# Three mask copies moved from VectorE to DMA, split output blocks at the end, and a new written-out order in a fused attention and gated-convolution kernel

## The chip, the cores and the metric

The kernel runs on one core of one Trainium2 chip. The core has five engines that run side by side, each strictly through its own list of instructions: TensorE (PE: matmuls and transposes), ScalarE (ACT: exponentials and other activations, copies), VectorE (DVE: elementwise work, copies), GpSimd (POOL: here the issue of the casting loads) and SyncE (SP: here the issue of the other DMAs). Engines wait for one another by semaphores. The metric is the device time of one execution in microseconds (us).

## The reference, cut to what matters

Block-sparse attention (4 batches, 8 heads, 768 tokens, head size 64, blocks of 32 tokens), and then a gated convolution feed-forward on the 512 wide result:

```python
scores = scale * q @ k.T
mask   = |blk_i - blk_j| <= 1, or first/last block on either side, or one of 3 sampled blocks of the query's block
attn   = softmax(where(mask, scores, -1e9));  x = attn @ v        # heads side by side: 4 x 768 x 512
h      = relu(x @ w_in)                                           # 512 -> 1024
conv   = sum over k of conv_w[k] * h shifted by k - 1 tokens      # 3 taps, per channel
out    = (h * sigmoid(conv)) @ w_out                              # 1024 -> 512
```

## The kernel before, in words

The 8 heads of a batch go as 4 pairs, so there are 16 pairs, P = 0 to 15. A pair's queries and keys lie transposed in a tile `T_t[slot]` of 88 rows by 24 columns of 128: rows 0 to 63 hold q and k, rows 64 to 87 hold the mask as 24 more "head elements" (a large negative number where a block pair is masked), so that one matmul over 88 rows gives the masked scores. There are five such slots. The mask rows are built once, in slot 0, by small DVE and ACT instructions at the start (`a1`, `a3`, `nblk`, `m_k`, `a4`, `a5`, `m_q0`, `m_q1`, `m_h1`, `m_r1`; lines 270 to 350), and copied from there into slots 1 to 4 by four VectorE copies `m_slot` (lines 354 to 357). Pair P uses slot P modulo 5 at first; pairs 1, 2, 3 are needed 4.5, 9 and 13.5 units after pair 0, pair 4 only 36 units after it.

The attention is 144 units. One unit is two `s` steps on TensorE (line 761: 1024 columns of scores into one of two PSUM tiles `st`), one `exp` on ScalarE (line 773: 128 x 1024 elements), and two `av` steps on TensorE (line 798). Every 18 units (one segment, half the tokens of a batch) the normalised rows (`rcp`, `norm`) are transposed (`x_tr` on TensorE or `x_xb` by DMA), multiplied with w_in (`f1`, line 895), cut at zero (`relu`, on ACT or DVE), convolved and gated on DVE with a `tanh` on ACT (`mul`, `add`, `tanh`, `g1`, `g2`), and multiplied with w_out (`f2`, line 830). A finished block of 128 tokens by 512 columns is copied out of PSUM by `ev` (ACT or DVE, function `dcopy`, lines 327 and 331) and stored by SP's `out` (line 839). Only the very last block, token block 5 of batch 3, is done in two halves of 256 columns, in the score tiles.

At the head, pair 0's q and k are loaded in fp32: q of head 0 first on ACT's queue, k of head 0 first on SP's. They are cast to bf16 (`cast_q`, `cast_k`), transposed on TensorE (`k_tr`, `q_tr`) and copied into slot 0 (`k_cp`, `q_cp`). Until the first scores TensorE is kept busy with 13 `warm` and 29 `fill` matmuls on zeros. All other loads go through POOL's casting queue, in a chain that is paced by tiny POOL copies (`pace`).

No scheduler decides the order: a function builds a list of 1787 operations with their choices of engine and of buffers, and the string `ORDER` (lines 20 to 62) gives, operation after operation, its number (two characters), the engine where there is a choice, and the buffers that it takes. `put_down` emits them so. The sequence of each engine is what this string leaves for it; the waits between engines follow from the data.

Of the kernel before, what the change touches and what calls it, by code (L numbers as in the profile page):

```python
# [21 lines left out]
1B01H10ZA0YA1CV01d1e1IA0+A13A0p0q1DV1E00r0s0t0u1FV1L01a1GV15V550560v0w0x5701yV165a15b0y0z0A0B2005c1222230C1J00D  # L22
0E0F0G1PA01Y12e11KV1S12a22g32h2s25f05g5h25k11V05l580595d1TV11UV1WV1XV5p05q0O1M15e1h05m35i5r4175y15z1i1n1NV1OV5j
5n5o21V15A55D05E2402715F05I15J5K10H25V228V29V26V5s5t15N05O5B5C5G5W15X5H5L5P25Y35u05v5/0602i1614641656655M5Q2l0
6906a2fV2186b05R5Z05+2jV32kV2mV2nV6e16f6g15w162636n0195S15T6o67686c6d6s16t5xV06p26u36h6x06y2u12tV36i16q6r4P2v4Q
2o34R1r2G04S2I01s1g4T2J4U6C16D6j26k6v1Z06l16z46L06M1l1p1+V6mV1/V6E51m1t4V2U14W1u4X2W24Y2X4Z1v4+6w6A6B6Q16R6F6N0
6G5U16S16V06W6X21w4/312506O06P6H06I6J05VV6T6+16/6KVih11k73074ii703ik01q2HV4ijV001o7547c17dil7e5in1ioipA17h07i
7m1imViF0iH7j0iGiIiq06U7n7o12b1ir2dV2cVisA7r06Y7s6Z7172767717A17B11iz1iA2Z07t27F07G7f7C32w0iBA2iJiN1iO7H4782iQ
797g7K12p12xV47L2rV2yV7k7l7p2qV7M57P07Q7qit02z17u7viP2BV2AV7w1iR7R07U17V7D0810iKiL7W12K12LV02MV7x82iuivV37E7I7J
7N8618733351347a17O7S7bV1832iS8838b07T7X7Z07Y18c7y08d4iT7+7zViM0iUiw1ixiyViV28g18h2Y1842N0858i58p08q8r0898a8u1  # L30
8v8e8f8j8k8w13522+361372OV2PViW8l28z08A8s08tiY8B27/18E18F8xiC08J08K8y80ViX8m8G38CiD8L48R18SiZ8T52VV0iEVj13j3j2
j918W08Xja8Y08n08D8H8/1908I9408M8oVi+8N1j42/V30Vj5911958U8V8Z8+jf096292jgi/j012j69c1j7j88O18P32V1939d9h09i97jh
jb9e49m19njijjV09j5jc9o139V38V523cjdA19r0989909a9s9w1jo0jp9t3jl11jjqA9x9E0jm9F3d13f9y09G2ju0jv3a0532C0542Q13e
9J19f09g3o3p03l3m1jwA9KjnVjJ0jK9k9O09P9l2D19pjL9L4jM2EV9Q5jr09q9ujs9vjN2FV3r3qjOjtVjR1jS3bV2jT9T19U9V1jA1jBjU
jx0jyjCAjzAjZ29/0a02R1a41a59z9B29A19H9I9M9N9R2TVa13a90aa9CjG08Q2j+jVk09ba602SAab2ae1afag4jD1jP9SjEjFVaj0akjH9W
jQj/jIVjk3h03t13i9D9Xa209Y19Za3k53k1al5jWa7a8acar1jXk6asaw0kj1axat3adahaiamaB1aCan1ay0auavazjYaD4k2kv0aG0aHk8
aI5k7k9ao0k3k4kaaO1kbkcaAkkaPaEaFkwaJaT0aKaL2aMaUkl3x3y23A3B2aQ1kxaY1aV29+3u3s4ap3g3aq03jV3kVkykzA2kmaZb103D3C
3Jb2knA3kB0kCkE1kFkDV14kGVkZ0k+a+3b303vVb61b7b84kN0kObe0aR1bfkQ1kRaSaWaXk/kPA5bj1bkkK0bg5kSAbl1l0l1l2kLbo0kW1a/
bpb0b4b5bt1b9buba0bq33M3N33K0aNbhld1kMVbv2kXbB0bCbikH0kYAbD03wVlf3nA3bG1kIbb1lelg3zV4bckT1bmbnbr3P3OkJV6bH3UbI4
3F03Q13Gl52l7kUkVV7l3bL0bMl6bN5kp0kqbsbwbxbQ1bRbS1bV0bWbdkokrkd1bE1bX33R3E0ll3lml8lol9lhlal41by0kAlblcbzlnlilp  # L40
ljc11ksbFbJbKbOc2c60c7c82ktA0bPbTbAkulk3IV3HVkekfkgc30cb0bUbYlt0lubZ0cccg1khA3lqlr3LV0b+2lscd4lvlz1chlAco0cplB
lCci5lwct1cuc4cq3lDA2lxA0cy0czc5lF13V23X3Y1403Zb/3+lGcv13SV13WV13TVlHVlI0lJcD1c9cElKVm10m2m3cacem4m5cA0cF2lO1cf
cI0cJcK4kilPlL0lMcjcklNAlQVm92ma410mbmcm6m7cl1cr1cQ1cRcS5cscwcV0cWcxcBcCcGcHlR0494a0c01ly4f1c+1c/cX13/46471cL
cN0mdd03lSd30d4lU1lVdb1dccOcmcncP42jelTAmelWVmh1mimjmfmkmgm84ed50dd2cM1cTcUcYcZlX0d1lYmllZVdg0dhdi4l+1l/dl1d2dm
d6d7dq0drm0Amp3de0d82dfdn54b4c4nds1mD1djdkdodpdv1dwdD0dEmx0mEmymmdx3mqd9msdtmrdudydz1dF2dI1dJmtmumnmo4o24s4ddG
dHdN0dOdK4mvmzmFdadP54kdS1dTdLmwmGdMd+0d/dQmA4pdA14l043V2mHV344VmBV0dU1e31dRe4e03dVdWdX0dBe52e80e9mV1mWea0mXV08
dYmY0mZe10e2m+Vnh0ninknjed1ee4glEn21e6m/0ei0ejn0n34B4C34qef4ek5n4A4Geq1ere7ebecegehelev04r4y4Des3n1V9np2nqnsnr
ewnl48V2en24hV3n50em1n6eteA1euex2n7Aa4t045dC2dZeBeon81mJ0eF0mKeGeC04z2n9mLnmeH4mMepeN1eOeS0eTmNA1naV4iV4mV34E4F
4MeP5ne1nb0nfeX1eyezeYeDeEeInx1nyntnzeU1nuf00eJncf1eZ34N14H1ngVnneK1eQ0eRmP1eVeWe+f514j4ueLeMf6f22ndAbe/f3fd0fe
f74mQmRnvno0nAnwnBnF3nGnInHfi1fjff5nCmC4vV4nD4wVnJf4mSmTA2nT0nUfn0fofk0f8f91fgo61o7fhfs1ftfp1fA0fBnK4Io8VnEmI  # L50
fu3nLfa0nMo31o4fC2flnVfmnWo5Vot0ouovowoxfb4AV4nXA0fF1fGfK0fLnN1nZ0nOfH4fM5oyfqfrnPn+n/AnQfP1fQo00fvo1nRA34JV0
4KVfwfU0fVoz4OV0oAfR0oc1g01g1o2AfW1fx2fyol2omfD0fEfIfJodonoog23opoeAg50g6g72o90oaga1fNfOfSgbfTfXfY1gf0ggobVoB1
oDoC4Loqgc4fZ1oi1ojof0ognS4xnYgh5orosoEf+g3g4gn1g8gogs0ohAokAoFoJ3oKg9gp0gtmUfc0fzoR0gu1oX1gdoLgegigx1gyoMoNoG
gjoSoHgG0gq0grgvgwgHoYgz3gAgBgL1gMoOgI2gk0oIglgC2gN4oToZgQ0gRgS5f/gmoPoQo+gJ1o/A3mOgZ1oUg+h20h3g/0h41p71p8p9pa
oVV0pbV2h71h8gKpg0phpd1p0pehg0gDgOpfV1cpiAhhh93pj0pm1pnhi2poAgPpkplAdhl1hmgThq0pp1gE0pqgUpB0pDpCpcpEpJ2pFhn4
gFA1h00h1h5h6haps0pthbprAepGpKpLpuAhrpMpv1hz1hApwhs5p10pHgV1gWhc0pNpxAfhB0hE0hdpR1pSpTpUp2gX1gYApOhj1hkp3p4hF
pI1pVp5A1hG1hohphthuhN1py1he0pzhv2pPhwhOhC0pQhfApAAhx0hDhHhW0hI1hyVqk1qlhP3hXpZ3hJ1p+p/pWqmAgqq0hQh/1qrhRq51hY2
i0i80i9q6q0q1pXhKq2qsAhpYhS0q3q4hL0q7hZ0q8i14ia5hMV2qh0qihTq9A3qB0qR2qCqDh+i2i31ibqn1qjAii42i5qt1qui60icid1qo
i7Aqb0qcqpAjqwqviehU1qdhVVif1qeigAri1rjqJ3qEqxqLqSqFqfA2r90raqyrkArbAqzqUrf1rgqGrc0rl0rmrhArA1rBp6qgoWqaqAqHqI
rn1qKrorC0rdr31rv0rwrDrpreArq1rrrEqTqMrx1rs0qZ0rtqNqOruryqVrzqPqQq+r4rR0rSrL1rMrNrOrTrUqWqXqYrPV1r5r6rVAr7A2q/  # L60
# [53 lines left out]
def kernel(  # L114
# [700 lines left out]

    def out_block(b, t, due, deps, after, tail=False, last=False):
        gb, ob = gt_buf[b], Buf(P_os)
        halves = ((0, 256), (256, 512)) if last else ((0, 512),)
        outs = []
        for x, (c0, c1) in enumerate(halves):  # L820
            mb = Buf(P_tail if last else P_mix)

# [4 lines left out]
            for a in range(4):
                def fn(e, a=a, acc=acc, c0=c0, c1=c1):
                    for ffc in (2 * a, 2 * a + 1):
                        nc.tensor.matmul(out=acc(), lhsT=gT_t[gb.index][:, ffc, 128 * t:128 * t + 128],  # L830
                                         rhs=woutb[:, ffc, c0:c1], start=(ffc == 0), stop=(ffc == NFFC - 1),
                                         skip_group_check=True)
# [224 lines left out]
```

## Time and profile before

| | |
|---|---|
| median of 3 runs | 208.67 us (208.65 to 208.9) |
| the profiled execution: span from first to last instruction | 206.8 us |
| what lies around the span, against the median | 1.9 us |
| PE, ACT, DVE, POOL busy | 199.3, 190.6, 186.4, 61.9 us |
| first `exp` starts, last `exp` ends | 7.61, 188.2 us |
| last matmul group starts, last copy out of PSUM ends | 199.4, 203.5 us |
| DMA | 25.2 MB, mean 122 GB/s |

The page shows the profiled execution by its span alone; its time is taken as this span and the 1.9 us around it. The page counts busy time by engine, gives the chain of work that ended last, and groups instructions by source line. A busy TensorE is not always one at its full rate, since the ends of its pipelined matmuls are modelled; its rate is better read from the chain of waits, where so many matmuls of one kind stand back to back with the time that they took.

### The profile page before, as it was taken

What the parts mean: (1) busy time and instruction counts of PE and PEld (TensorE: products, weight loads), DVE (VectorE), ACT (ScalarE), POOL (GpSimd) and SP (SyncE); (2) the same over time, 40 slices, a digit from 0 to 9 for tenths busy, and PEclk for the clock granted to TensorE, in tenths of its full rate; (3) what the DMA queues carried; (4) which work ended last, traced back from release to release, by engine and by line L of the source; (5) the groups of instructions that cost most, each with busy time, mean ns of one, the idle gap of its engine ahead of it and who ended that gap; (6) DMA issues with size and microseconds to landing.
All of it is one profiled execution on the core that took longest, in us unless ns stands there. A gap on an engine that the chain in (4) does not pass through costs nothing.

```text
span 206.8 us, 6250 instructions
## 1 busy us (share of the span) xinstructions
PE 199.3 (96%) x2418; PEld 142.7 (69%) x2418; DVE 186.4 (90%) x576; ACT 190.6 (92%) x252; POOL 61.9 (30%) x113
## 2 busy tenths in 40 slices
...
GB/s 156 196 196 185 181 165 132 187 113 77 78 127 142 179 102 93 147 139 193 194 96 107 138 77 170 151 144 130 67 115 87 22 120 51 3 51 5 152 53 153
DMA packets 49305, 25.20 MB, mean 122 GB/s; under 512 B 35100, under 2 KB 46332, under 8 KB 49276
## 3 DMA queue, kind: packets, MB, share of 16 engines
...
q10 hardware_dynamic: 288, 0.30, 0.4%
...
## 4 chain that ended last, share of the span: by engine, by line
PE 71%; DVE 14%; ACT 11%; issue 2%; ACTq 0%
PE st L761 22%; PE mix L830 18%; PE mix L895 16%; PE av L798 12%; ACT pt L773 8%; DVE t L331 3%; DVE m L953 3%; DVE m L961 2%; DVE gT L1008 1%; ACT t L327 1%; DVE xtok L709 1%; PE st L830 1%; DVE hE L917 1%; PE mix L728 1%; DVE m L1003 1%
## 5 line engine op out<-in xcount | busy, mean ns | idle before, releaser
L773 ACT ACTIVATE pt<-st 128x1024 bf16<-128x1024 f32 x144 | 140.6, 1048 | 2.4 <-PE st L761 1.3
L761 PE MATMUL st<-t 88*128 88x256 bf16 (+2 forms) x600 | 90.0, 267 | 1.6 <-ACT t L327 0.8
L761 PEld LDWEIGHTS <-t 88*128 88x128 bf16 x600 | 48.5, 97 | 21.4 <-issue 1.6
L798 PEld LDWEIGHTS <-pt 128*128 128x128 bf16 x1152 | 52.2, 97 | 11.5 <-ACT pt L773 1.0
L798 PE MATMUL av<-vt,pt 128*128 128x65 bf16 x1152 | 58.4, 193 | 0.0
L895 PE MATMUL mix<-xT,winb 128*128 128x384 bf16 (+2 forms) x288 | 54.3, 308 | 0.3 <-ACT hE L915 0.2
L953 DVE TENSOR_SCALAR m<-hE,cw 128x382 bf16<-128x382 bf16 (+2 forms) x192 | 48.8, 316 | 0.4
L830 PE MATMUL mix<-woutb,gT 128*128 128x512 bf16 x184 | 48.7, 379 | 0.2 <-DVE gT L1008 0.2
L961 DVE TENSOR_TENSOR m<-m 128x764 bf16<-128x764 bf16 (+2 forms) x64 | 33.8, 534 | 0.6
L895 PEld LDWEIGHTS <-winb 128*128 128x128 bf16 x288 | 24.4, 97 | 9.4 <-issue 0.8
L1000 ACT ACTIVATE m<-m 128x764 bf16<-128x764 bf16 (+2 forms) x32 | 26.8, 840 | 1.1 <-DVE m L961 1.0
L407 POOL COPY pace<-pt 1x1 bf16<-1x1 bf16 x24 | 9.6, 402 | 53.3 <-ACT pt L773 53.3
L830 PEld LDWEIGHTS <-gT 128*128 128x128 bf16 x200 | 17.3, 97 | 11.7 <-DVE gT L1008 1.1
L915 ACT ACTIVATE hE<-mix 128x384 bf16<-128x384 f32 (+2 forms) x36 | 17.7, 507 | 1.7 <-PE mix L895 1.6
L917 DVE TENSOR_SCALAR hE<-mix 128x384 bf16<-128x384 f32 x28 | 15.5, 557 | 4.1 <-PE mix L895 3.7
L1008 DVE TENSOR_TENSOR gT<-m,hE 128x764 bf16<-128x764 bf16 (+3 forms) x36 | 18.2, 511 | 0.6
L709 DVE TENSOR_TENSOR xtok<-av,rcp 128x384 bf16<-128x384 f32 (+2 forms) x36 | 18.1, 508 | 0.5
L239 POOL DMA_DIRECT2D nat<-in_q_dram x23 | 17.0, 738 | 2.1 <-issue 1.4
L331 DVE COPY t<-mix 64x384 bf16<-64x384 bf16 (+1 forms) x33 | 13.4, 413 | 0.7 <-PE mix L522 0.2
L327 ACT COPY o2s<-mix 128x512 f32<-128x512 f32 x17 | 9.9, 598 | 2.9 <-PE mix L830 2.7
L1003 DVE TENSOR_SCALAR m<-m 128x764 bf16<-128x764 bf16 (+3 forms) x36 | 12.1, 335 | 0.5 <-ACT m L1000 0.4
L239 POOL DMA_DIRECT2D vn<-in_v_dram x15 | 11.3, 756 | 1.9 <-DVE vt L331 1.4
...
## 6 DMA issues: line engine op xcount, KB each, us to landing
...
```

The costliest lines, as they stand in the source:

```text
L239: return op(name, {eng: occ}, lambda e: on(e).dma_start(out=dst(), in_=src), prio, deps, dma=(kind, service), **kw)
L331: nc.vector.tensor_copy(out=dst, in_=src)
L709: nm = op("norm", {"DVE": t_dps(128 * C)}, lambda e: nc.vector.tensor_tensor(out=xtok_t[xk.index][:, 0:C].rearrange("p c h d -> p h c d"), ...
L761: nc.tensor.matmul(out=st[:, 128 * x:128 * (x + n_)], lhsT=t[0:88, 12 + 6 * hh + kc, :], rhs=t[0:88, idx:idx + (n_ - 1) * (2 if P < NPE el ...
L773: nc.scalar.activation(out=pt_t[ptb.index][:, c0:c1], in_=st_t[stb.index][:, c0:c1], func=AF.Exp, bias=0.0, scale=0.125)
L798: nc.tensor.matmul(out=o[:, off:off + 65], lhsT=pt_t[ptb.index][:, 128 * x:128 * x + 128], rhs=V_t[vslot_b[P].index][:, hh, kc, 0:65], sta ...
L830: nc.tensor.matmul(out=acc(), lhsT=gT_t[gb.index][:, ffc, 128 * t:128 * t + 128], rhs=woutb[:, ffc, c0:c1], start=(ffc == 0), stop=(ffc == ...
L895: nc.tensor.matmul(out=mix_t[hb.index][:, w1 * y:w1 * y + w1], lhsT=winb[:, fc, 128 * ffc:128 * ffc + 128], rhs=xT_t[xt_buf[n].index][:, f ...
L953: nc.vector.tensor_scalar(out=m_t[cb.index][:, x, y, 0:w], in0=hE_t[heb.index][:, f0 + y, t0 + x:t0 + x + w], scalar1=cw[:, x, f0 + y:f0 + ...
L961: nc.vector.tensor_tensor(out=m[:, a_, :, 0:w], in0=m[:, a_, :, 0:w], in1=m[:, b_, :, 0:w], op=ALU.add)
L1000: th = [op("tanh", {"ACT": t_act(2 * w) + 0.04}, lambda e, cb=cb, w=w: nc.scalar.activation(out=m_t[cb.index][:, 0, :, 0:w], in_=m_t[cb.in ...
L1008: nc.vector.tensor_tensor(out=gT_t[gtb.index][:, f0:f0 + 2, t0:t1], in0=m_t[cb.index][:, 0, :, 0:w], in1=hE_t[heb.index][:, f0:f0 + 2, 1 + ...
```

## The change

First, `m_slot` stays a VectorE copy for slot 1 alone. For slots 2, 3 and 4 it becomes a DMA on SP's queue, `m_sp`, from slot 0's mask rows to the other slot's, 24 rows of 6144 bytes each (147 KB).

Second, blocks 3 and 4 of batch 3 are now also computed and stored in halves of 256 columns, as block 5 was. That makes 8 `f2` steps (32 matmuls of 256 columns in place of 16 of 512), 2 `ev` and 2 `out` more. These halves stay in the `mix` PSUM tiles.

Third, the whole `ORDER` is replaced (1799 operations). What it changes at the head, engine by engine (loads that the engine only issues are left out):

| engine | before | after |
|---|---|---|
| DVE | 3 fillers, memsets, a1, a3, nblk, m_k, ident24, m_h1, a4, a5, a5, k_cp ... | memsets, cast_q (head 0), a1, nblk, a3, m_k, ident24, a4, a5, k_cp, m_q0, cast_q, k_cp, m_h1, a5, q_cp, cw, m_q1, m_r1, m_slot, v_cp (pair 0), q_cp (pair 1), k_cp (pair 1) ... |
| ACT | m_k, cast_q, cast_k, cast_k, m_q0, m_q0, q_cp, m_q1, m_h1, exp 0, exp 1, v_cp (pair 0), exp 2, exp 3 ... | m_k, cast_k (head 1), cast_k (head 0), m_h1 (24 x 768), k_cp, q_cp, m_q0, k_cp, exp 0, exp 1, exp 2, k_cp and q_cp (pair 1), exp 3 ... |
| PE | 13 warm, 10 fill, k_tr 0, q_tr 0, 2 fill, k_tr 1, 4 fill, s 0, s 1 ... | 13 warm, 4 fill, k_tr 1, 7 fill, k_tr 0, q_tr 0, 11 fill, s 0, s 1, q_tr 1 ... |
| SP | mask to `mback` (2 DMAs), xb, m_turn ... | m_sp slot 2, mask to `mback` (2 DMAs), m_sp slot 3, m_sp slot 4, m_turn, xb ... |

On POOL both w_in loads now come before pair 4's q. Later in the run, ACT has 11 copies `o2s<-mix` of 512 columns where it had 17, and DVE 10 where it had 6; ACT no longer does the two `v_cp`, and DVE one `relu` fewer. In the last stretch TensorE ends with block 4 left, block 4 right and block 3 right, where it ended with block 3, block 2 and the whole block 4; the last copy is one of 256 columns on ACT.

```diff
 ORDER = """
-0J0K1c1f00021010P0Q1Q01R0R0S0T0310V0/A0U14V1b0I0L0M0N0V0W0X1xA11zA1AA0405060708090a0b0c0d0e0f0g0h0i0j0k0l0m0n0o
...
+00021030405060I0L0M0N0O010708090P0Q1Q01R0R0J0K1L00a1xV10R1b0T0S10V1d0U1a2000b0c0d0e0/A1AA0f0g0h0i1E00j0k0l0m0n0o0p1zA
...
 """
...
     for s in range(1, NSLOT):
-        mr = [op("m_slot", {"DVE": 0.95}, lambda e, s=s: dcopy(e, T_t[s][64:88], T_t[0][64:88]),
-                 T(4.5 * s - 2.5), m_h1 + m_r, earliest=7.0 + 2 * s)]
+        if s == 1:
+            mr = [op("m_slot", {"DVE": 0.95}, lambda e, s=s: dcopy(e, T_t[s][64:88], T_t[0][64:88]),
+                     T(4.5 * s - 2.5), m_h1 + m_r, earliest=7.0 + 2 * s)]
+        else:
+            mr = [dma("m_sp", "SP", lambda s=s: T_t[s][64:88].rearrange("j c s -> j (c s)"),
+                      T_t[0][64:88].rearrange("j c s -> j (c s)"), T(4.5 * s - 2.5), m_h1 + m_r, service=0.3)]
         mask_ready[(s, 0)] = mask_ready[(s, 1)] = mr
...
     def out_block(b, t, due, deps, after, tail=False, last=False):
         gb, ob = gt_buf[b], Buf(P_os)
-        halves = ((0, 256), (256, 512)) if last else ((0, 512),)
+        halves = ((0, 256), (256, 512)) if last or (b == B - 1 and t > 2) else ((0, 512),)
...
-                due + 3, [evo], uses=[ob], dma=("hw", 0.65 if not last else 0.4)))
+                due + 3, [evo], uses=[ob], dma=("hw", 0.65 if len(halves) == 1 else 0.4)))
```

More of the change, by code (lines that the diff above doesn't have):

```diff
@@ L20 @@
 ORDER = """
-0J0K1c1f00021010P0Q1Q01R0R0S0T0310V0/A0U14V1b0I0L0M0N0V0W0X1xA11zA1AA0405060708090a0b0c0d0e0f0g0h0i0j0k0l0m0n0o
[L22 to L60, printed above, removed]
@@ new lines @@
+5T1m6n06o1Z11+V2tV36p26c6d6s16t6x06y6h6j26k1/V6i16q6u36z46r6C16D6v6w6l06L06M6A6B5U15VV1g6mV6E56Q16R6F6G6N06S11w4/
+312506V06W6O06P6X26H06I1k6J16KV6+16/6T6Uih073074703ii7c17dik17547e5il7h02HV41qijV00imViF0iGiHiI7i7j0in0io7m17niq16Y
+6ZipA17o12b0ir7r07s712cV2dViJisA727t2iK762p17717A17BiN12qV2rV2w02xV47F07G7f7g7k7l7piO7822yV79iP7C37H4iz17q7uiA7K17L
+iBA27M57v2z07P07Q7D07E7I2K17U17V7w1iQ2AV2BV7R07J7N7O81082it07W133351342LV0iR2MViLiu86187iw17Six832iS883ivV37xiM0iyV
+7T7X7Z02VV08b08c7Y18d484852N08g18h8i57+2OV2PV898a7a18p08q7y08eiV27bV1iX7zViT2Y12Z02+iW2/ViY361352373g38r08f8u18v8j
@@ new lines @@
+7/18w18k8z08AiC08s08E18F8t8B28x8y8G38C8J08KiD8D8L48l280V8miZ32V1iEViU30Vj138R18S8T5j918W08X8Y08H8I8n08M8/1ja90940
+8N18U8V95i+8O1j28oVj3j4i/j538Vj039V911962j6jf0jg8Z8+929c19d939e4523a0533c3d12C03f543e9h09i97jbjh98j79m19nj8jijc990
+8P1jjjV09j39o59r09f09sjdA19t09w1jl0jm9xjo19a123bV2jnVjp9E0jqV9F9y19G2ju0jv9g9J19K2Q13l3o3p03m13r9k9l2D19O09PjwAjJ0
+jKjLjM9L49Q32EVjNjO2FV9pjr0js9q9ujtV9v9T19U9z9A19H9/0a0jA1jBjx09I9MjyjR19B2jSjTjU9C9V5a10a41a5jCAjzAa612R1a909Naa9R
+9S9W9Xa20ae1af3h08Q23q3i3t13u9bab2jVjZ22SVj+j/a3jG0jHaj0a7a8jP2TV9Y1k0ag4jWjIVakjD1acadahar1asal3aijEat0jQ9ZjXk1jFV
@@ new lines @@
+jYaw0aman1kj0axauaB1kv1aCkkk2ay1aG0aHavaD4kwazaAaO1aEaPaFaI3k53k6k7ao0k8k9kaaQ1aT0aJaKaUk3k4aV4klkx9+3s49Dkbkc3jVap
+3vVaL13A3B23x3D3M3N33y23CaY1kykzA2aZkmknV3b10a+5aR0b2kB1b32kCb61kE0kF3wVkDV14kGV3kVkZ0k+l0aMb7b803P3J3K0be0kH1bfkN0
+kOaSaWaXbj1a/kPA5b0kIb4b5bkb9kJV6bb2bg1bck/ba1bhbo0kQ0bpkRkSVbl3bq4bibmbt1bukW1bB0kXkK0bCbnbv5kYAld1le3nV3lglfbD2kL
+bG1brbHbI0bsbwkT1kUbL0bMkVA7bxbE0aq0je3E03F1aN3Q03Okojk3G3RbdbN1bFbQ1kp1kMVl1l52l23zV4ll3lhkd0bRbV0bJbKbObPkqbWkr
+bS3lic11bTksc2bX5ktA1c32l6lmby0lnl7l8bzl3l9l41lj3LV0lolklalbkebUbYkfc60lc3HVbAkuc7lz1cb1cckgbZ1c4c5c803X3Y13U3V140
```

26 lines of the change are left out of this document (25 added, 1 removed).

## The prediction

> **What bounds the kernel now.** I read the page first, then a table by stretches, cut at the first exp (7.61), at exp 24 (31.35), at exp 48 (57.86), and at the tail.
>
> ```profile
> PE 199.3 (96%) x2418; PEld 142.7 (69%) x2418; DVE 186.4 (90%) x576; ACT 190.6 (92%) x252; POOL 61.9 (30%) x113
> PE 71%; DVE 14%; ACT 11%; issue 2%; ACTq 0%
> ```
> ```profile
> core 0: us, PE busy (x) PEld busy (x) DVE busy (x) ACT busy (x) POOL busy (x), PEclk, DMA share, GB/s
> 0.00:7.61 7.61, 5.67 (x48) 4.43 (x49) 6.11 (x29) 5.21 (x11) 6.42 (x14) 1.00 0.77 169
> 7.61:31.35 23.74, 22.98 (x325) 18.02 (x324) 22.21 (x69) 23.66 (x26) 15.06 (x27) 1.00 1.26 183
> 31.35:57.86 26.51, 26.23 (x374) 19.85 (x373) 25.99 (x75) 26.36 (x31) 10.83 (x22) 1.00 1.08 116
> 57.86:190.00 132.14, 131.81 (x1571) 92.66 (x1570) 121.55 (x365) 127.44 (x167) 29.61 (x51) 1.00 0.73 111
> 190.00:203.54 13.54, 12.57 (x108) 7.73 (x106) 10.58 (x42) 7.91 (x18) 0.00 (x0) 1.00 0.33 117
> ```
>
> Three engines are nearly full. From the first exp to exp 48, ACT is busy 50.02 of 50.25 us: its list sets the pace, and whatever delays the first exp delays exp 48 by as much. Behind exp 48, ACT and DVE have air (92 to 97% up to 190) and PE has hardly any. How near PE is to its full rate comes from the chain of waits, where groups stand back to back:
>
> ```profile
> 57.54 0.44 PE st L761 x4
> 79.78 1.30 PE mix L895 x8
> 187.68 0.87 PE mix L895 x8
> 188.56 0.48 PE av L798 x16
> 197.69 1.75 PE st L830 x16
> 199.44 3.50 PE mix L830 x16
> ```
>
> Behind 57.86 stand 96 units (0.44 of scores and half of 0.48 of av each: 65.3 us), f1 with 192 matmuls of 384 columns (1.30/8: 31.2), 32 of 256 (0.87/8: 3.5) and 32 of 128 (half of that: 1.8), f2 with 168 of 512 columns (3.50/16: 36.7) and 16 of 256 (1.75), and some 2.4 of transposes and convolution: 142.6 us. They took from 57.86 to 202.94, 145.1. So PE loses only 2.5 us there; that is all that a better order can win behind exp 48, the split of the last blocks aside.
>
> **The head, where the new order decides.** In the new list `cast_q` of head 0 is DVE's third instruction, ahead of everything that builds the mask. It needs a load. These rows of the timeline show the mask work of before, all run while that load was in flight, and ACT's list behind it.
>
> ```profile
> 1.22 0.17 DVE L271 CAST apart<-apart_i 24x24 f32<-24x24 int32 x1
> 1.69 0.17 DVE L274 TENSOR_SCALAR A<-A 24x24 f32<-24x24 f32 x1
> 2.37 0.55 DVE L286 COPY nblk<-ident 24x768 bf16<-24x768 bf16 x1
> 2.96 0.70 ACT L327 COPY t<-nblk 24x384 bf16<-24x384 bf16 x1
> 3.69 1.23 ACT L327 CAST nat<-o2s 128x192 bf16<-128x192 f32 x3
> 5.54 0.60 ACT L327 COPY t<-mtok 24x128 bf16<-24x128 bf16 x2 [0.63 <-DVE mtok L299]
> 6.17 0.47 ACT L327 COPY t<-mix 64x384 bf16<-64x384 bf16 x1
> 6.69 0.60 PE L761 MATMUL st<-t 88*128 88x384 bf16 x4 [0.78 <-ACT t L327]
> 7.08 0.50 ACT L327 COPY t<-t 24x384 bf16<-24x384 bf16 x1
> 7.61 1.94 ACT L773 ACTIVATE pt<-st 128x1024 bf16<-128x1024 f32 x2
> 8.06 0.26 DVE L331 CAST nat<-o2s 128x192 bf16<-128x192 f32 x1
> 8.36 0.95 DVE L331 COPY t<-t 24x3072 bf16<-24x3072 bf16 x1
> 9.57 0.83 ACT L327 CAST vt<-m 128x768 bf16<-128x768 f32 x1
> ```
> ```profile
> q10 hardware_dynamic: 145, 0.11, 13.1%
> ```
>
> The last row is ACT's DMA queue in the window 0 to 3.0: 0.11 MB, of which this load (96 KB, 0.098 MB) is the first. So it lands hardly before 2.9, and by 3.69, when ACT casts it now. I take 3.6, near the late end, as a load counts as landed behind its slowest part. Then, with those durations:
>
> DVE: cast 0.26, a1 0.64 (1.22 to 1.86), nblk 0.55: nblk ends at 5.1 where it ended at 2.92. ACT's first copy needs nblk: 0.70, to 5.85. Two casts of the three that took 1.23: some 0.9, to 6.75. `m_h1` of 24x768, newly on ACT: between 0.50 (24x384) and 0.83 (768 elements), taken 0.8 as nearest in elements, to 7.5. `k_cp` and `q_cp`, 0.45 each, and `m_q0`, 0.30: to 8.75. The scores start at 8.8 (before 6.69) and the first exp 0.6 later, at 9.4; before it was 7.61, held by two mask copies on ACT that are now on DVE. The 12 more fills ahead of the scores end before 8.8 and cost nothing as long as ACT is this late.
>
> Then three exps at 0.92 bring ACT to 12.15; `k_cp` of pair 1 (64x768, as the 0.83) and `q_cp` (0.47), overlapped 1.2, stand ahead of exp 3, and `v_cp` (0.83) no longer does: exp 3 at 13.4. Of before the ACT rows are:
>
> ```profile
> 10.31 20.65 ACT L773 ACTIVATE pt<-st 128x1024 bf16<-128x1024 f32 x22
> ```
>
> Exp 2 to 23 took 20.65, so exp 3 began near 11.23 and 0.94 each. The lag from exp 3 on is 13.4 - 11.23, taken 2.1. With the load at 2.9 and `m_h1` at 0.5 it is 1.1; if `q_cp` waits for DVE's own list (m_slot 0.95, v_cp, q_cp ahead of it), 2.6.
>
> Between 31.35 and 57.86 ACT has the same list as before, 26.36 busy of 26.51: 0.15 at most comes back. **The lag at exp 48: +2.0.**
>
> **The mask copies.** DVE loses 3 x 0.95 = 2.85 us between 8.4 and 31. That is off the path: in this stretch ACT sets the pace, and the DVE copies are spent again on casts and evictions (below). SP gains 3 DMAs of 147 KB. They need m_r1, which DVE reaches near 11.1, so slot 2's is issued at 11.2. A landing of 147 KB on SP's queue is not shown; the nearest rows:
>
> ```profile
> m<-in_v_dram SPq DMA_DIRECT2D x1, 384.0 KB, 7.2
> xT<-xtok SPq DMA_TRANSPOSE x20, 3.2
> ```
>
> Between 3.2 and 7.2 (the head's traffic, more bytes): 14.4 to 18.4, taken 16. Unit 9's scores, the first to need it, come 1.3 ahead of exp 9, at 16.8 + 2.1 - 1.3 = 17.6. Cost nothing, at the upper end 0.8. Behind it SP's two mback issues (0.9 each) hold slot 3's copy to 13.6; it lands by 20.8, needed at 21.4. Slot 4's is wanted 36 units in. Traffic of 0.44 MB at 183 GB/s delays the loads in flight by up to 2.4, about what the lag gives them in time: nothing. m_turn ahead of xb on SP: pair 6 is wanted at unit 45, past 54 us; hidden by 10 us. The w_in loads ahead of pair 4's q: pair 4 is wanted at unit 36, past 44; hidden likewise.
>
> **Behind exp 48.** ACT gives up 6 copies of 512 columns and takes 2 of 256, gives up one v_cp, q_cp and x_cp, takes a relu; DVE takes 4 of 512, 2 of 256, q_cp and xT copies, and gives up 2 relus.
>
> ```profile
> L327 ACT COPY o2s<-mix x17: 586/587/646, 57.2 to 203.0; 128x512 f32<-128x512 f32 x17
> L327 ACT COPY o2s<-st x1: 372/372/372, 199.5 to 199.5; 128x256 f32<-128x256 f32 x1
> L331 DVE COPY o2s<-mix x6: 680/692/693, 57.0 to 201.2; 128x512 f32<-128x512 f32 x6
> ```
>
> ACT: -6 x 0.59 + 2 x 0.37 - 0.85 - 0.47 - 0.4 + 0.5, about -4.0. DVE: 4 x 0.69 + 2 x 0.42 + 0.9 - 2 x 0.56, about +3.4. On neither is that the path; PE is, and its matmuls are the same (32 of 256 columns cost 3.5, as 16 of 512 do). The gain is the share of PE's 2.5 lost us that a freer ACT brings back: at most 2.5; below nothing too, as DVE, fuller by 3.4, holds PE where it did not (-0.6). I take 0.8, a third: by the table PE stands idle only 0.33 up to 190 and 0.37 from there to 202.94, and the rest is matmuls that run slower than back to back, which a freer ACT mends only in part.
>
> **The tail.** The last copy is 256 columns on ACT, 0.37 for 0.59, and its DMA half as long.
>
> ```profile
> 202.95 0.59 ACT L327 COPY o2s<-mix 128x512 f32<-128x512 f32 x1 [1.97 <-PE mix L830]
> GB/s 384 344 405 344 364 61 0 0 0 0 0 0 0 0 202 384 445 364 364 364 384 81 0 0 0 0 0 0 0 0 0 0 0 0 0 0 0 0 0 0
> ```
>
> In the last 4.05 us (slices of 0.1) the last block's bytes take some 0.75; half of them 0.35 less (0 to 0.4). The two extra `out` issues go at 0.33 each under matmuls. Together -0.5.
>
> **Sum:** 206.8 + 2.0 - 0.8 - 0.5 = 207.5 of span; with the 1.9 between span and median, 209.4. The own range of this course: lag 1.1 to 2.6, PE's share 1.5 to 0, tail -0.2 to -0.6: 208.9 to 210.9.
>
> **Rivals.**
>
> *PE gives the lag back: faster.* Place: behind exp 48. The lag is at its low end, 1.3, and ACT's 4.0 us lets PE win 2.0 of its 2.5: 206.8 + 1.3 - 2.0 - 0.5 = 205.6, 207.5 as a median. It decides from where lag minus PE's gain falls under 0.1. For it: waits of PE for ACT and of ACT's copies for PE stand in the tables of waits. Against: near all of a loss would have to come back. Chance 0.22.
>
> *The two cancel.* Lag 1.6, gain 1.1, tail 0.5: 208.7. Chance 0.13.
>
> *Slot 2's mask is late.* It lands behind 17.6, and scores, av and exps all stand behind the waiting scores on PE. At the upper end, with the lag at 2.6 and DVE's -0.6: 206.8 + 2.6 + 0.8 + 0.6 - 0.5, as a median 212.2; by half of these 211. Chance 0.10.
>
> *PE's clock drops in the longer pause at the start.* After 13 warm and 4 fill PE waits for ACT's cast from 4.3 to 6.4, where before it waited 0.78 at most (the row of the scores above). That PE ran at half rate at first is in the rows by form:
>
> ```profile
> L230 PE MATMUL av<-warm 128*128 128x256 bf16 x13 | 3.0, 419 | 1.2 <-DVE warm L223 1.2
> L761 PE MATMUL st<-t 88*128 88x256 bf16 x216 | 39.9, 272 | 0.0
> ```
>
> 256 columns took 419 ns, later 272. If that comes back for the 3 us that it lasted at first, three units of 0.68 PE time (0.44 + 0.24) become 1.36, 0.42 over the 0.94 of an exp: 1.3 us, 210.7. Chance 0.05. The Trainium skill, page "TensorE: Matmul & The Clock Gate", section "Part 1: The HAM clock gate", says that the array falls back to half clock after an idle window of about 3.4 us; by its figure a pause of 2.1 us is too short unless the thin work around it counts as idle, and nothing in this trace shows a pause that long.
>
> **How the numbers follow.** Likeliest course 0.50, at 209.4; the rivals 0.22, 0.13, 0.10 and 0.05. A measurement of this kernel tells about 0.2% (0.4 us) from no change. Faster by more: 0.22; within: 0.13; slower: 0.65. For 8 in 10 the range takes half of the fast rival (from 207.6) and reaches to the late mask's middle case: 207.6 to 211.2.
>
> **What would show it.** Right: DVE idle before its third instruction until about 3.6; nblk ending near 5.1; first exp at 9.4 (8.5 to 9.9), exp 3 at 13.4, exp 48 at 59.9; the last copy 0.37. Wrong: a first exp before 8.3 (the load lands early); exp 48 later by under 1.2; a wait of PE for a DMA into `t` near 17; from exp 48 to the last copy clearly under 144 us, which would be the fast rival.

## The result, and the profile after

The changed kernel takes 213.89 us (median of 4 runs, 213.01 to 215.38) beside 208.69 us (208.65 to 208.9): a ratio of 1.0255, 95% interval 1.0216 to 1.0294. It is slower by 5.2 us; the forecast was slower by 0.7. The span of the profiled execution is 212.2 us, 5.4 more.

The page of after, its busy times and its chain by engine:

```profile
PE 201.9 (95%) x2434; PEld 146.2 (69%) x2434; DVE 186.3 (88%) x581; ACT 188.9 (89%) x246; POOL 58.4 (28%) x113
PE 57%; DVE 25%; ACT 8%; DMA 7%; issue 2%; SPq 0%; ACTq 0%; DVEq 0%
```

ACT's busy time fell by 1.7 us and DVE's by 0.1, while the span grew: the loss is waiting. The table by stretches of after, cut at the same exps as before (0, 24 and 48) and in the tail, shows where:

```profile
core 0: us, PE busy (x) PEld busy (x) DVE busy (x) ACT busy (x) POOL busy (x), PEclk, DMA share, GB/s
0.00:11.05 11.05, 7.58 (x49) 5.56 (x50) 6.66 (x28) 5.44 (x9) 8.40 (x17) 1.00 0.97 179
11.05:36.67 25.62, 22.69 (x322) 18.02 (x323) 18.80 (x65) 23.61 (x27) 12.46 (x26) 1.00 1.11 166
36.67:64.27 27.60, 27.20 (x379) 20.38 (x378) 27.15 (x82) 27.13 (x33) 10.28 (x21) 1.00 0.86 120
```

The first exp starts at 11.05 for 7.61 (+3.4). The next stretch, exp 0 to 24, takes 25.62 for 23.74 (+1.9), with ACT idle 2.0 us where it was idle 0.1. Exp 24 to 48 takes 27.60 for 26.51 (+1.1); here ACT is as full as before, but has one relu more (three of 0.50 where there were two) and waits 0.4 once for DVE. So exp 48 starts 6.4 us later (64.27 for 57.86). Part of this last step is only a matter of place: the new order puts exp 48 later among ScalarE's other work, and exp 72 is 5.9 us late again. Exp 143 starts at 193.71 for 187.16, 6.5 later, and only what follows it is shorter, 18.5 us to the end of the span for 19.6. Nearly the whole loss is made by exp 9, which is already 6.0 us late. The timeline of after there (start, duration, engine; in brackets the idle time ahead and what ended it):

```profile
3.43 0.37 DVE L330 CAST nat<-o2s 128x192 bf16<-128x192 f32 x1 [2.35 <-DMA o2s<-in_q_dram]
4.68 0.85 DVE L285 COPY nblk<-ident 24x768 bf16<-24x768 bf16 x1
5.56 0.69 ACT L326 COPY t<-nblk 24x384 bf16<-24x384 bf16 x1 [2.63 <-DVE nblk L285]
6.28 0.92 ACT L326 CAST nat<-o2s 128x384 bf16<-128x384 f32 x2
6.85 0.50 PE L463 MATMUL av<-ident,nat 128*128 128x128 bf16 x3 [2.41 <-ACT nat L326]
7.14 0.95 PE L229 MATMUL av<-warm 128*128 128x128 bf16 x7
8.80 1.35 PE L229 MATMUL av<-warm 128*128 128x128 bf16 x11
9.95 1.06 PE L764 MATMUL st<-t 88*128 88x384 bf16 x4
11.05 1.02 ACT L776 ACTIVATE pt<-st 128x1024 bf16<-128x1024 f32 x1 [0.85 <-PE st L764]
12.90 0.18 DVE L374 TENSOR_SCALAR cw<-mix 128x24 f32<-128x24 f32 x1 [0.97 <-PE mix L372]
16.09 0.48 ACT L326 COPY t<-mix 64x384 bf16<-64x384 bf16 x1 [0.92 <-DVE t L330]
16.59 5.62 ACT L776 ACTIVATE pt<-st 128x1024 bf16<-128x1024 f32 x6
```

One chain runs through the engines: DVE waits 2.35 us for the load of q, ACT 2.63 for DVE's `nblk`, PE 2.41 for ACT's cast. Then PE is busy, but slow: four score matmuls take 1.06 where they took 0.60, three transposes 0.50 where they took 0.33. The clock column says 1.00 throughout, but the trace of after holds a record of the clock only from 12.14 on (that of before from 4.36 on), and where it holds none the column says 1.00. So the rate has to be read from matmuls of one kind. Minimum, median and maximum duration in ns of the filler matmuls (the last ones ahead of the first transposes in before; the last ones ahead of PE's pause and the first ones behind it in after), the form with 128 columns:

```profile
L230 PE MATMUL av<-warm x7: 219/219/284, 4.2 to 4.6; 128*128 128x128 bf16 x7
```
```profile
L229 PE MATMUL av<-warm x5: 314/314/421, 3.6 to 4.1; 128*128 128x128 bf16 x4, 128*128 128x256 bf16 x1
L229 PE MATMUL av<-warm x4: 314/314/314, 7.1 to 7.5; 128*128 128x128 bf16 x4
```

The 421 ns are those of the one matmul with 256 columns. The records of neighbouring matmuls overlap, so the rate is the distance from start to start: seven fillers of after take 0.95 us together (row at 7.14), so one starts every (0.95 - 0.314) / 6 = 0.106 us. PE of after stays at this rate, that of its first microseconds, until about 12: it had not risen when the pause began at 4.44, and did not rise in it. The mask copies show in its chain of waits:

```profile
14.25 7.73 DMA t<-t
22.11 0.61 PE st L764 x4
22.80 0.64 ACT pt L776
```

Slot 2's copy is issued at 14.25 and lands 7.73 us later; the scores of unit 9 and exp 9 wait for it (0.6 us). At the end of the kernel, the last copy of after:

```profile
209.16 0.37 ACT L326 COPY o2s<-mix 128x256 f32<-128x256 f32 x1 [0.50 <-PE mix L833]
```

### The profile page after: what moved, and what is told of

Its sections match the earlier page's. It is cut to its first block, busy times and chain, and to the rows that moved or that the text cites. A ratio compares the mean times of both kernels' runs of the same rounds, so it can differ in the third digit from the quotient of the medians.

```text
span 212.2 us, 6287 instructions
## 1 busy us (share of the span) xinstructions
PE 201.9 (95%) x2434; PEld 146.2 (69%) x2434; DVE 186.3 (88%) x581; ACT 188.9 (89%) x246; POOL 58.4 (28%) x113
## 3 DMA queue, kind: packets, MB, share of 16 engines
q0 software_dynamic: 19728, 11.05, 43.8%
## 4 chain that ended last, share of the span: by engine, by line
PE 57%; DVE 25%; ACT 8%; DMA 7%; issue 2%; SPq 0%; ACTq 0%; DVEq 0%
PE st L764 16%; PE mix L898 14%; PE mix L833 13%; PE av L801 9%; DVE m L956 7%; ACT pt L776 6%; DVE t L330 6%; DVE m L964 4%; DMA t<-t 4%; DVE xtok L712 2%; DMA stg<-nat 2%; DVE hE L920 1%; DVE gT L1011 1%; DMA o2s<-in_q_dram 1%; DVE m L1006 1%
## 5 line engine op out<-in xcount | busy, mean ns | idle before, releaser
L764 PE MATMUL st<-t 88*128 88x256 bf16 (+2 forms) x600 | 94.0, 269 | 1.8 <-DMA t<-t 0.8
L801 PEld LDWEIGHTS <-pt 128*128 128x128 bf16 x1152 | 55.4, 97 | 15.1 <-issue 1.3
L801 PE MATMUL av<-vt,pt 128*128 128x65 bf16 x1152 | 62.4, 193 | 1.1 <-DVE vt L330 1.1
L898 PE MATMUL mix<-xT,winb 128*128 128x384 bf16 (+2 forms) x288 | 55.5, 307 | 0.3 <-DVE o2s L330 0.2
L833 PE MATMUL mix<-woutb,gT 128*128 128x512 bf16 (+1 forms) x200 | 49.3, 362 | 0.5 <-DVE gT L1011 0.3
L833 PEld LDWEIGHTS <-gT 128*128 128x128 bf16 x216 | 18.9, 97 | 10.6 <-DVE gT L1011 1.5
L410 POOL COPY pace<-pt 1x1 bf16<-1x1 bf16 x24 | 7.1, 297 | 57.9 <-ACT pt L776 57.7
L920 DVE TENSOR_SCALAR hE<-mix 128x384 bf16<-128x384 f32 x27 | 14.8, 552 | 2.9 <-PE mix L898 2.8
L330 DVE COPY t<-stg 64x1536 bf16<-64x1536 bf16 x20 | 12.2, 608 | 0.3
L238 POOL DMA_DIRECT2D nat<-in_k_dram x15 | 10.8, 723 | 3.3 <-DMA nat<-in_k_dram 1.5
```

The lines of the kernel that those rows point to most:

```text
L238: return op(name, {eng: occ}, lambda e: on(e).dma_start(out=dst(), in_=src), prio, deps, dma=(kind, service), **kw)
L330: nc.vector.tensor_copy(out=dst, in_=src)
L764: nc.tensor.matmul(out=st[:, 128 * x:128 * (x + n_)], lhsT=t[0:88, 12 + 6 * hh + kc, :], rhs=t[0:88, idx:idx + (n_ - 1) * (2 if P < NPE el ...
L801: nc.tensor.matmul(out=o[:, off:off + 65], lhsT=pt_t[ptb.index][:, 128 * x:128 * x + 128], rhs=V_t[vslot_b[P].index][:, hh, kc, 0:65], sta ...
L898: nc.tensor.matmul(out=mix_t[hb.index][:, w1 * y:w1 * y + w1], lhsT=winb[:, fc, 128 * ffc:128 * ffc + 128], rhs=xT_t[xt_buf[n].index][:, f ...
```

## The experiments

Theory A, from the trace: the loss is the head's order, through the first cast's wait, and PE's half rate is a part of it. Rivals: B, the mask transfers; C, the order behind the head; D, the half rate is only a companion of the wait and costs nothing. "After" and "before" name the kernel that was edited; orders are shown as operation names by engine. The table has each run's median, its ratio to before as measured beside it, and how much later than in before the numbered exp starts in its profiled execution. That execution is one of the run's own and need not be a typical one: that of x5 took 211.03 us, 1.1 above the median, that of x2 211.57, 0.8 below it.

| run | median us | ratio (95%) | exp 0 | exp 3 | exp 9 | exp 48 | exp 143 |
|---|---|---|---|---|---|---|---|
| after | 213.89 | 1.0255 (1.0216 to 1.0294) | +3.4 | +5.4 | +6.0 | +6.4 | +6.5 |
| y1_cast_third | 213.69 | 1.0243 (1.0225 to 1.0261) | +3.7 | +5.2 | +5.2 | +5.3 | +5.4 |
| x1_cast_later | 210.88 | 1.0114 (1.0092 to 1.0136) | +0.7 | +2.3 | +2.4 | +2.9 | +3.0 |
| x5_cast_cw_later | 209.96 | 1.0063 (1.0038 to 1.0087) | +0.7 | +1.7 | +2.0 | +3.5 | +3.6 |
| x2_more_fill | 212.41 | 1.0173 (1.0149 to 1.0197) | +2.3 | +3.4 | +3.4 | +4.1 | +4.2 |
| y5_no_fill | 210.16 | 1.0068 (1.0050 to 1.0086) | 0.0 | +0.5 | +1.9 | +1.9 | +1.9 |
| x7_cast_later_fill10 | 210.86 | 1.0097 (1.0071 to 1.0124) | +0.3 | +2.1 | +2.9 | +3.7 | +3.9 |
| x3_slot_dve | 214.24 | 1.0273 (1.0242 to 1.0305) | +3.1 | +4.6 | +5.5 | +6.9 | +7.0 |
| x4_both | 212.14 | 1.0169 (1.0125 to 1.0213) | +0.4 | +2.1 | +4.1 | +5.5 | +5.6 |
| x8_cw_slot_dve | 211.81 | 1.0157 (1.0126 to 1.0189) | +0.8 | +1.5 | +2.8 | +4.2 | +4.3 |
| y2_msp | 215.95 | 1.0355 (1.0321 to 1.0388) | 0.0 | 0.0 | +7.0 | +6.9 | +6.6 |
| y2b_msp | 209.64 | 1.0077 (1.0046 to 1.0107) | 0.0 | 0.0 | 0.0 | +1.3 | +1.1 |
| w1_head_before | 208.57 | 0.9991 (0.9981 to 1.0000) | 0.0 | 0.0 | -0.1 | +0.6 | +0.7 |
| y3_tail_half | 208.20 | 0.9982 (0.9973 to 0.9991) | 0.0 | 0.0 | 0.0 | -0.1 | -0.1 |
| w3_tail_after | 208.03 | 0.9971 (0.9961 to 0.9982) | 0.0 | 0.0 | -0.1 | 0.0 | +0.3 |

### The first cast's place

```diff
 y1_cast_third (before)
-ACT: ..., m_k, cast_q (head 0), cast_k, cast_k, ...
-DVE: warm_mem, ident_mem, ...
+ACT: ..., m_k, cast_k, cast_k, ...
+DVE: warm_mem, ident_mem, cast_q (head 0), ...
 x1_cast_later (after)
-DVE: ..., cast_q (head 0), a1, nblk, a3, m_k, ident24, a4, ...
+DVE: ..., a1, nblk, a3, m_k, ident24, cast_q (head 0), a4, ...
```

> The kernel before with one operation moved: the cast of head 0's q goes from ScalarE to VectorE as its first work behind the two memsets, as in the changed kernel. Theory (this place alone costs most of the loss): nblk ends at 5.0 to 5.6, first exp at 10 to 11 (7.61), the lag stays through exp 48, the time 211 to 212. Rival (it costs only together with the rest of the new head): first exp at 8.6 or earlier, the time under 210.

> The changed kernel with one operation moved: the cast of head 0's q stands on VectorE behind ident24, where it stood third. Theory (the early cast holds the whole head): nblk ends near 2.9 again, ScalarE starts its copies at 3.0, TensorE's pause before the first transpose shrinks from 2.4 to about 0.4 us, so its matmuls run at full rate, and the first exp comes at 7.6 to 8.2 where it came at 11.05. What stays is the copy into slot 2 on SP and the longer ScalarE list before exp 3: exp 9 at 18 to 19 (22.80), the time 209 to 210.5. Rival (the rest of the new order and the copies on SP are what costs): first exp earlier, but exp 48 still 4 us or more later than in the kernel before, the time 212 or more.

Put alone into before, this one operation's place costs 5.1 us, nearly all of it by exp 3; that is more than was expected (213.69 us beside 211 to 212), and PE at half rate (granted clock 0.50 from 8.6 to 15.5 us in its trace) is a part of it. Taken out of after, it gives back 3.0 of 5.2, a little less than expected (210.88 beside 209 to 210.5): so it is the largest cause, and in after's order other delays lie beside it that it partly hid. What is left in x1 is in its chain of waits ahead of exp 3:

```profile
2.57 7.07 DMA cw<-in_moe_conv_w_dram
9.68 0.25 PE mix L373
9.95 0.19 DVE cw L375
11.23 0.95 DVE t L331
13.07 0.48 ACT t L327
```

DVE's list has `cw`, the conversion of the convolution weights, ahead of the copies that exp 3 needs, and the load of the weights ends only at 9.64. DVE waits, and ACT's `q_cp` behind it.

```diff
 x5_cast_cw_later (after, beside the edit of x1)
-DVE: ..., cw, diag, diag, ..., q_cp (pair 0, second half), ...
+DVE: ..., q_cp (pair 0, second half), cw, diag, diag, ...
```

> The kernel with the cast moved (run x1), and beside it the transpose and the scaling of the convolution weights (cw) moved behind the second half of pair 0's q, with the two diag groups that need them. In x1 the chain before exp 3 runs from the load of the convolution weights (lands at 9.6) through cw on VectorE to m_q1, m_r1, m_slot, v_cp, q_cp and from there to ScalarE's q_cp, which stands ahead of exp 3. Theory (that chain is what is left of the loss): exp 3 comes at 11.8 to 12.8 instead of 13.57, the time 209.2 to 210.2 (210.88). Rival (ScalarE's two copies ahead of exp 3 cost it by themselves): exp 3 within 0.3 of 13.57 and the time within 0.4 of x1.

That gives 0.9 us more, and is 1.4 above the before measured beside it. Exp 3 is now 1.7 late instead of 2.3. The rest was not divided further; the trace of x5 has ACT wait 0.47 for DVE ahead of exp 3, where the cast of v, which ACT did before, now stands on DVE ahead of the copy.

### PE's half rate

```diff
 x2_more_fill (after)
-PE: 13 warm, 4 fill, k_tr 1, ...
+PE: 13 warm, 48 fill, k_tr 1, ...
 y5_no_fill (before)
-    NWARM, NFILL = 13, 29
+    NWARM, NFILL = 13, 0
 x7_cast_later_fill10 (after, beside the edit of x1)
-PE: 13 warm, 4 fill, k_tr 1, ...
+PE: 13 warm, 10 fill, k_tr 1, ...
```

> The changed kernel with 44 more fill matmuls on zeros ahead of the first transpose, so that TensorE doesn't pause while VectorE waits for the load. Theory (a part of the loss is TensorE at half rate after the pause): transposes, fills and scores at the head run at 56 ns for 128 columns instead of 107, the first exp at 9.5 to 10.0 instead of 11.05, exp 3 at 14.5 to 15.5 instead of 16.59, the time 1.0 to 2.0 us shorter: 212 to 213. Rival (ScalarE's and VectorE's lists alone hold the head): first exp within 0.3 of 11.05, the time as it is, 213.9.

> The kernel before without its 29 filler matmuls (a part of the work that no result uses); nothing else is changed. If a thin stretch of PE work ahead of about 5 us is by itself enough for half rate, the first score matmuls take about 0.85 instead of 0.44 us for four, exp 0 starts 0.5 to 1.2 us later, exp 9 lags 1 to 2.5 us, and the time is 209.7 to 211.2 although no wait was added. If the filler is without effect and the half rate of after came from the delay alone, the time is 208.5 to 208.9.

> After with the first cast behind the identity work on DVE, and six more filler matmuls ahead of the first transposes (ten, as before has). If PE's first stretch of work, cut from 23 matmuls to 17, is what leaves the head at half rate in the run with the cast later alone (210.88), the filler matmuls behind the first transposes take 0.219 us and not 0.314 from about 4.7 us on, and the time falls by 0.3 to 1 us to 209.9 to 210.6. If the half rate does not bind there (the scores wait for ACT's copies anyway), the time stays at 210.6 to 211.2.

With 44 more filler matmuls in its pause, after wins 1.5 us, though no wait between the engines is taken away. With all 29 taken out of before (16 of them stand ahead of the first scores, 13 behind), before loses 1.5 us, though no such wait is added. These are the timeline of x2 and the windows of y5 (stretch, length, PE busy, clock, DMA):

```profile
6.93 0.33 PE L465 MATMUL av<-ident,nat 128*128 128x128 bf16 x3
7.10 0.55 PE L231 MATMUL av<-warm 128*128 128x128 bf16 x7
9.32 0.60 PE L766 MATMUL st<-t 88*128 88x384 bf16 x4 [0.49 <-ACT t L328]
```
```profile
7.00:8.00 1.00, 0.72 (x8) 1.00 1.47 195
8.00:9.00 1.00, 0.61 (x5) 0.50 1.23 187
13.00:15.00 2.00, 2.00 (x22) 0.54 1.37 195
15.00:17.00 2.00, 2.00 (x38) 1.00 1.42 190
```

In x2 the same work runs at full rate again: the seven fillers take 0.55 us, one from start to start (0.55 - 0.219) / 6 = 0.055 us, half of the 0.106 in after. In y5 the clock is recorded: half from 8 on, and 22 matmuls in the 2 us from 13 on for 38 in the next 2. There exp 0, expected 0.5 to 1.2 late, was still on time, and the delay came behind it, 1.9 us by exp 9. So D falls: the half rate costs about 1.5 us by itself. x7 is a miss: six more fillers brought the first exp forward by 0.3 us, but the time stayed. In its trace PE falls to half rate later, around 12.6, after it has waited 1.21 us for DVE's `vt`; a longer start did not help here, where the other engines leave PE little to do later.

The list alone does not fix the rate behind the pause. x3 (below) has the same lists up to the first copy between slots on SP, at about 14 us. In its trace PE paused for 2.78 us, from 4.44 to 7.22, came back at full rate and fell at 8.2; these are its fillers on both sides of the fall:

```profile
L230 PE MATMUL av<-warm x7: 219/219/219, 7.4 to 7.7; 128*128 128x128 bf16 x7
L230 PE MATMUL av<-warm x8: 314/314/314, 8.7 to 9.5; 128*128 128x128 bf16 x8
```

So the trace of after and that of x3 show two courses of one head, with the first exp at 11.05 and at 10.72.

### The mask copies

```diff
 x3_slot_dve (after), x4_both (with the edit of x1), x8_cw_slot_dve (with the edits of x5)
-        if s == 1:
-            mr = [op("m_slot", {"DVE": 0.95}, ...
-        else:
-            mr = [dma("m_sp", "SP", ...
+        mr = [op("m_slot", {"DVE": 0.95}, ...
 y2_msp, y2b_msp (before): the same lines the other way round
-SP: ld_k0, ld_sb, ld_q0, ld_v0, ld_cw, mback, mback, ...
 y2_msp
+SP: ld_k0, ld_sb, ld_q0, ld_v0, m_sp, m_sp, m_sp, ld_cw, mback, mback, ...
 y2b_msp
+SP: ld_k0, ld_sb, ld_q0, ld_v0, ld_cw, m_sp, m_sp, m_sp, mback, mback, ...
```

> The changed kernel with the three mask copies back on VectorE, where they stood in the order before, and none on SP. Theory (the copy into slot 2 lands late): TensorE's wait of 0.85 us for a DMA into t near 22 is gone, exp 9 lags by 5.4 and not by 6.0, and VectorE hides its 2.85 us because ScalarE sets the pace: the time 0.4 to 0.9 us shorter, 213.0 to 213.5. Rival (taking the copies off VectorE is worth its 2.85 us): the time 1 to 3 us longer.

> The kernel before with only the first part of the change: the mask copies into slots 2, 3 and 4 as transfers on SP, issued as soon as slot 0's rows are ready (about 8.4). Theory (ScalarE sets the pace here, so VectorE's 2.85 us are worth nothing, and a landing of 5 to 8 us puts slot 2 at 14 to 16 where it is wanted at 15.4): 208.5 to 209.5, with a wait of TensorE for a DMA into t at the upper end. Rival (VectorE, 94% busy from 8 to 31, is what limits): 0.5 to 2 us shorter, 206.7 to 208.2.

y2 measured something else than it was made for. The three issues wait on SP for the mask rows, and the load of the convolution weights stood behind them: issued at 10.58, for 2.54 in before. Its chain of waits:

```profile
7.60 1.03 ACT pt L777
8.63 0.38 SPq L239
9.05 0.73 SPq L239
9.82 0.71 SPq L239
10.58 6.99 DMA cw<-in_moe_conv_w_dram
17.62 0.30 PE mix L373
18.25 0.85 PE st L765 x4
```

PE waited 5.4 us for it with all scores behind, and came back at half rate (0.85 for four score matmuls, otherwise 0.44). The waiting issue held the load behind it. y2b mends that.

> The kernel before with the mask copies of slots 2 to 4 as SBUF transfers on SP, this time with the load of the convolution weights ahead of them on SP, so that nothing else stands behind their wait. If the earlier loss of 7.4 us came from the weights held up behind the waiting issues, it is gone here: issues at about 8, 9 and 10 us, landings 6.4 to 7.7 us later at 14.5, 16 and 17.5, against DVE copies that ended at about 14 to 18; exp 0 and exp 3 with no lag, exp 9 within 1 us, time 208.0 to 209.6. If the transfers themselves are what costs (late landing for slot 2, whose scores are wanted at about 15.4), exp 9 lags 2 us or more and the time is 210 or more. If freeing 2.9 us of DVE is worth something, the time is under 208.3.

Alone in before, with only the mask's own two transfers to `mback` close behind them, they cost 1.0 us. The executions spread widely: seven of 209.2 to 210.5 us at a mean granted clock of 0.996 or more, three of 210.9 to 212.0 at 0.988 to 0.992. Neither of the two ways that were expected to show the cost is the one: exp 9 is on time, so slot 2's rows come early enough. ACT first waits two exps later, behind a load. The issues of before (first row) and of y2b (the others) between 8 and 18 us, with their median time to landing where it is given, and two pieces of y2b's chain:

```profile
nat<-in_k_dram POOLq DMA_DIRECT2D x2, 192.0 KB, 5.5
```
```profile
t<-t SPq DMA_DIRECT2D x3, 144.0 KB
nat<-in_k_dram POOLq DMA_DIRECT2D x2, 192.0 KB, 8.7
9.77 8.82 DMA nat<-in_k_dram
18.64 0.51 PE mix L464 x6
```

DMA is busy throughout this stretch (190 GB/s in before, all 40 slices from 8 to 18 us at 90% or more). Beside the three transfers of 147 KB (144.0 KB in the rows, which count 1024 bytes to the KB) the loads of keys take 3.2 us longer to land, and PE's transposes of the next pair wait 1.1 us for one of them. In after's order the sign is not the same. With the first cast left third, DVE copies and transfers differ by less than the intervals (x3, 214.24 for 213.89): the wait for the DMA into `t` is gone, as expected, and exp 9 is 0.5 us earlier, but exp 48 is 0.5 later, and neither the expected gain of 0.4 to 0.9 nor the rival's loss of 1 to 3 came. With the cast moved, DVE copies are slower than transfers by 1.3 us (x4 for x1, intervals overlapping a little) and 1.9 (x8 for x5).

> After with the first cast behind the identity work on DVE and the mask copies of slots 2 to 4 back on DVE. If the transfers cost about 1 us whatever the head (input loads land later, slot 2 lands late), 210.88 falls to 209.6 to 210.3. If DVE's list in the head is what binds, the three copies of 0.95 us return what the transfers took and the time stays at 210.5 to 211.5 or rises.

> The same with the conversion of the convolution weights moved behind pair 0's second q half as well (209.96 with the transfers on SP). If the transfers are the rest of the loss, this gives 208.6 to 209.3; if the order of DVE's list is the rest, 209.6 to 210.6, with exp 9 still about 2 us later than before.

Both go against the idea that the transfers are the rest of the loss. The waits of x8 between 10 and 30 us say why:

```profile
PE st L761 <- DVE t L331: 2.3, 2, 1.6
ACT pt L773 <- PE st L761: 2.1, 2, 1.3
```

DVE's list of after leaves no room for the copies where I put them back; other places were not tried, so the 1.3 and 1.9 hold for these. B falls as the cause of the loss; in these runs the transfers are a trade between DVE time and DMA time, a loss in before's order and a gain in after's once the cast is moved.

### The order behind the head, and the halves

```diff
 w1_head_before: order of before to exp 23, of after behind it; m_slot on DVE; blocks 3 and 4 in halves
 w3_tail_after: the same, cut at exp 131
 y3_tail_half (before)
-        halves = ((0, 256), (256, 512)) if last else ((0, 512),)
+        halves = ((0, 256), (256, 512)) if last or (b == B - 1 and t == 4) else ((0, 512),)
```

> The order of the kernel before up to exp 23, mask copies on VectorE included, and behind it the order of the changed kernel with the halves at the end. Theory (all of the loss lies in the head): exp 24 within 0.3 us of the kernel before, and the rest gains the tail's half microsecond: 207.5 to 208.7. Rival (the new order is worse behind the head too): 209.5 or more, with the lag growing behind exp 24.

> The kernel before with only the last block in the order, block 4 of batch 3, in halves of 256 columns: 8 f2 steps for 4, the left half copied by VectorE, the right by ScalarE, two DMAs of 128 KB. Theory (the split saves the difference of the last copy, 0.59 to 0.37, and part of the last transfer): 0.3 to 0.6 us shorter, 208.1 to 208.4. Rival (the last transfer's time is latency and the matmuls of 256 columns cost as much more): within 0.2 of 208.7.

> The kernel before in its own order up to exp 131 (mask copies on DVE), and the order of after behind that, with blocks 3 and 4 of the last batch in halves. If the halves are the gain and the tail's new order is as good or better, the time is 207.9 to 208.3 (block 4 in halves alone gave 208.20); if the order of after's tail costs something by itself, 208.6 or more. All starts up to exp 131 as before.

With before's head, after's order is as fast as before: theory C falls, and the whole loss of 5.2 us is in the part up to exp 23, the mask copies with it. The lag was expected within 0.3 us at exp 24 and was -0.7 there, then +0.6 at exp 48 and +0.1 at exp 72: the order only moves these exps among the other work. The halves alone win 0.4 us (0.18%). After's order from exp 131 on, with both blocks in halves, wins 0.6 (0.29%, interval 0.18 to 0.39%). Against w3, w1 suggests that after's order between exp 23 and exp 131 costs about 0.5 (the two intervals just touch). w3, the kernel before with after's tail alone, is the fastest of all, ahead of both kernels.

## Why the prediction was wrong

The direction and the place were right; the time was 4.5 us too low, outside the range. Nearly all of it is the lag, 6.4 at exp 48 where 2.0 was summed: of the missing 4.4 us, 1.65 arose by exp 0, another 1.6 by exp 3, 0.6 by exp 9 and 0.5 after that. The bounds given for the likeliest course add up to 207.7 to 211.1, not to 208.9 to 210.9; the result lies above either.

**The cast's wait: right.** DVE idle until 3.43 (taken 3.6). `nblk` ended at 5.53 and not 5.1, as it took 0.85 here and 0.55 before.

**"The scores start at 8.8 ... and the first exp 0.6 later, at 9.4", and "the 12 more fills ... cost nothing": the step that failed first.** Each PE operation was costed at its rate of before. The scores started at 9.95 and the first exp at 11.05, outside 8.5 to 9.9. With PE kept busy (x2) the first exp came at 9.95; the 0.55 that is then left is mostly `nblk`. So 1.1 of the 1.65 us is the half rate. This was the rival with a chance of 0.05. Its size was right: 1.3 us was worked out, 1.5 was measured both by filling the pause and by thinning PE's work in before. Its mechanism was nearly right: in the trace of after PE did not drop in the pause; its first stretch, of 17 matmuls, ended at 4.44 without a rise to full rate. Its chance was too low, since I weighed the pause against a rule of 3.4 us of idle time and not against the thin work on both sides: in y5 PE fell at 8.0 though none of the pauses between its matmuls was above 1.1 us. The Trainium skill, page "TensorE: Matmul & The Clock Gate", section "Part 1: The HAM clock gate", says that the window of about 3.4 us runs freely and does not reset when the kernel starts. The traces agree: with one and the same first stretch of PE work, full clock is first recorded at 4.36 us in before, at 4.97 in y3 and at 5.88 in y2b; and with nearly equal pauses (2.41 us in after, 2.42 in y1), PE came back at half rate in after, and in y1 at full rate, to fall at 8.6.

**Exp 3 at 13.4, lag 2.1 (1.1 to 2.6): mis-sized.** It measured 5.4; with PE at full rate (x2) still 3.4. I listed "`q_cp` waits for DVE's own list" as the upper end; it was the case, and the list was longer than counted, as `cw` in it waits 0.97 us for PE (row at 12.90), in x1 for its load; moving it behind `q_cp` gave 0.9 us (x5).

**"The same list as before, 0.15 at most comes back" between exp 24 and 48: wrong.** The list has a relu more and the lag grew by 1.1 us there. But w1 shows the same step of 1.3 us (-0.7 to +0.6) by this order alone, and both give 0.5 of it back by exp 72: mostly a matter of place, not of time lost.

**The mask copies, "Cost nothing, at the upper end 0.8": wrong.** The issue came at 14.25 (11.2 taken), the landing after 7.73 us, above my bounds of 3.2 to 7.2. Exp 9 waited for it, 0.6 us. That follows from the late head: in x1 the copy is issued at 11.29 and its last packet ends at 16.18, almost the 11.2 and 16 of the working, and nothing waits for it. Alone in before the copies cost 1.0 us, and by the term that I set to nothing: loads in flight, slower by 3.2 us where I had bounded it by 2.4. In after itself, taking the copies back to DVE changed nothing that could be measured (x3).

**Behind exp 48, -0.8, and the tail, -0.5.** From exp 48 to the last copy's start 0.2 came back (its lag is 6.2 after 6.4), and the tail gave 0.8: the copy 0.2, and from its end to the end of the span 2.6 for 3.2. Together -1.0 for -1.3: the sum was near, its parts were not.

**The signs.** DVE's wait and the last copy of 0.37 were as named. The wait of PE for a DMA into `t`, named as a sign of error, stood there at 22 instead of 17. The rivals "faster" and "cancel" needed a lag near 1.5; it was four times that.
